# State's part of linear attention with 128 columns of weights on two row halves of the array

## The chip, the cores and the metric

The kernel runs on one core of one Trainium2 chip. The metric is the device time of one execution in microseconds (us), given as the median of several runs. One further execution was taken by the hardware profiler; the profile and the trace are of that one.

## The reference

Two stages follow each other. The first is causal linear attention with a decay for each head, over blocks of the sequence; the second mixes positions with a low-rank product and then runs a two-layer network on the channels.

```python
# q, k, v: (4, 8, 768, 64); lam: one decay for each of 8 heads
for b in range(nb):
    intra = einsum('bhic,bhjc->bhij', qb, kb) * Dmask
    intra = einsum('bhij,bhjd->bhid', intra, vb)
    inter = einsum('bhid,bhde->bhie', qb * lam_pow, kv_state)
    out[:, :, sl] = intra + inter
    kv_state = lam_block * kv_state + einsum('bhsd,bhse->bhde', kb * rev_pow, vb)
...
x = out.transpose(0, 2, 1, 3).reshape(B, S, H * D)      # (4, 768, 512)
xt = x.transpose(0, 2, 1)
u = x + (xt @ U @ V).transpose(0, 2, 1)                 # rank 32
return u + maximum(u @ w_ch1, 0) @ w_ch2                # 512 -> 2048 -> 512
```

All data are float32.

## The kernel before

The attention walks over 24 chunks of P = 128 positions (4 batches of NT = 6 chunks); `s` is the chunk, `c = s % NT` its place in the batch. All 8 heads of a chunk are worked on together, as HP = 4 pairs `a` of two heads `x`. In transposed tiles head `2a + x` of a pair lies on the partitions `half[x]`, that is 0 to 63 or 64 to 127. The kernel takes blocks of 128 positions where the reference takes 64, which gives the same sums.

For each chunk TensorE does this:

- `prep` (L358): transposes of q and k into `pqk`, copied by ScalarE (ACT) to `qt` and `kt` (L364).
- `scores` (L406): for each of 8 heads one product `kt` by `qt`, 64 rows of the array by 128 columns of weights, 128 moving columns, into the two PSUM banks of `pss`, bank `x` for the row half `x`. VectorE (DVE) multiplies by the mask (`masked`, L415) to `sm`.
- `intra` (L447): `sm` by `v` into `px`, with 64 columns of weights at a time (`t` is the half of the 128 positions).
- `state` (L425): `ks` by `v`, the sum for the next chunk, into `pkv`; DVE adds the faded old state and writes `kv` (L433).
- `inter` (L458): the part that comes from the state, `qs` (q times powers of the decay, made by GpSimd, L390) by `kv`, added into the same `px`. It is left out in the first chunk of a batch, where there is no state: 20 of the 24 chunks have it. Then ACT copies `px` to `x_nat` (L464).

`px` has two banks, one for each `x`; within a bank there are the 4 pairs by 64 output columns. `intra` starts the sums in a bank and `inter` adds to them.

Between these come the transposes and mixes of earlier chunks (L608, L559), and at the end of a batch the low-rank product (L474). The order is written by hand: `pieces` lists the functions chunk by chunk, and within one chunk TensorE runs, from the second batch on, `prep` of the next chunk, L608, L559, `intra`, `state`, `inter`, and `scores` of the next chunk. In the first batch `state` stands before `intra`. After the last chunk `inter` is followed by the first product of the network (L817) in place of scores. All loads and stores are issued by SyncE (SP): q, k and v from `load` (L279), where a new load waits until its buffer is free.

The attention fills the first 117 us. The rest of the time is the network: L817 and L827 for the first layer, L950, L952 and L954 for the second.

A float32 product is two instructions of TensorE and two weight loads, so the trace shows two records for each product of the attention. In the notation of the profile, "64*64" is rows by columns of the part of the array that a record uses, and PEld are the weight loads.

Of the kernel before, what the change touches and what calls it, by code (L numbers as in the profile page):

```python
# [18 lines left out]
def kernel(  # L19
# [28 lines left out]
    nc = tc.nc  # L48

    B, H, S, D = q.shape  # L50
    HP = H // 2
# [283 lines left out]
    st = {}  # L335
    kv = {}
    half = [slice(0, D), slice(D, P)]
# [114 lines left out]
    def inter(s):  # L452

        px = st[s]["px"][:, :, 0 : HP * D].rearrange("p x (a e) -> p x a e", a=HP)
        for a in range(HP if s % NT else 0):
            for x in range(2):
                for t in range(2):
                    nc.tensor.matmul(  # L458
                        out=px[half[t], x, a, :], lhsT=st[s]["qs"][half[x], a, half[t]],
                        rhs=kv[s][half[x], a, :], start=False, stop=(a == HP - 1),  # L460
                    )
        pool, tag = (att, "x10") if s % 10 == 5 else (x_pool, "x")
        xs[s] = pool.tile([P, C], FP32, tag=tag, name="x_nat")
        nc.scalar.copy(xs[s].rearrange("p (a x e) -> p x a e", a=HP, x=2), px)  # L464
        del st[s]
# [204 lines left out]
    def load_next(name, engine=nc.sync):  # L670
# [3 lines left out]

    run = {
        "prep": prep, "fade": fade, "scores": scores, "masked": masked, "inter": inter,
        "intra": intra, "state": state,
        "low": low, "low_rows": low_rows, "next_of_low": next_of_low, "mix": mix, "turn": turn,
# [375 lines left out]
```

## Time and profile before

| what | value |
|---|---|
| median of 3 runs | 667.36 us (666.33 to 668.0) |
| profiled execution, device time | 669.62 us |
| its span, first to last instruction | 667.8 us |
| granted TensorE clock | 1.00 |
| TensorE idle for "issue", 20 to 215 us | 4.0 us (1.6, 0.9, 0.8 and 0.7) |
| `inter` (L458), matmul records | 640, busy 14.7 us |
| `scores` (L406), matmul records | 384, busy 29.1 us |
| first product of the network (L817) starts | 117.36 us |

Busy time is the union of the records of a group; the ends of matmul records are modelled, so successive records overlap, and the time that a group costs is read from the start of its first record to the start of the next group's first. "Idle" is the time that the engine stood before a group, with what ended it; "issue" means that nothing in the profile explains it.

### The profile page before, as it was taken

How to read it: one execution, taken by the hardware profiler on the slowest of the kernel's cores; microseconds unless marked ns; L12 is line 12 of the kernel's file. 1: busy time of each engine (PE TensorE's matmuls, PEld its weight loads, DVE VectorE, ACT ScalarE, POOL GpSimd, SP SyncE). 2: the span in 40 equal slices, each digit the busy share in tenths (PEclk: the TensorE clock that was granted, in tenths of full speed). 3: DMA queues.
4: the chain of work that ended last, by engine and by line, in shares of the span. 5: the costliest groups of instructions: out<-in, count | busy, mean ns of one | idle time of the engine just before them, and what ended most of it. 6: DMA issues, size and time to landing. Idle time of an engine off the chain costs nothing.

```text
span 667.8 us, 13404 instructions
## 1 busy us (share of the span) xinstructions
PE 656.2 (98%) x5242; PEld 538.7 (81%) x5242; DVE 491.0 (74%) x862; ACT 280.4 (42%) x530; POOL 115.0 (17%) x98
## 2 busy tenths in 40 slices
PE   8899999999999999999999999999999999999997
PEld 7788988788888888888888887888888888888886
DVE  5578988878999777777797255786677776865864
ACT  4677885554555444444453121332322322322320
POOL 4465876330000000000000000030030300300300
PEclk9999999999999999999999999999999999999999
DMA  8999984355776655555578899764263453543531
GB/s 197 224 224 233 259 217 139 127 190 162 268 249 238 216 199 202 201 201 200 201 263 292 311 326 395 253 212 126 89 211 104 125 190 94 168 147 96 159 93 63
DMA packets 131776, 131.29 MB, mean 197 GB/s; under 512 B 81346, under 2 KB 89794, under 8 KB 131714
## 3 DMA queue, kind: packets, MB, share of 16 engines
q1 hardware_dynamic: 130512, 130.05, 62.2%
q8 instruction: 41, 0.67, 0.4%
q10 hardware_dynamic: 1202, 0.39, 0.2%
q14 instruction: 21, 0.17, 0.1%
HBM read 80.09 MB, written 50.33 MB: 195 GB/s over the span
## 4 chain that ended last, share of the span: by engine, by line
PE 95%; DMA 1%; DVE 1%; SPq 1%; issue 1%; ACT 0%; DVEq 0%; ACTq 0%
PE pz L817 27%; PE pz L950 13%; PE pz L952 13%; PE pd L827 13%; PE pd L954 13%; PE px L447 3%; PE pss L406 3%; PE px L458 2%; PE pqk L358 2%; DMA qraw<-in_q_dram 1%; PE pkv L425 1%; SPq L279 1%; PE pp L474 1%; PE pm L559 1%; PE put L590 1%
## 5 line engine op out<-in xcount | busy, mean ns | idle before, releaser
L817 PE MATMUL pz<-u_hl,w 128*128 128x512 f32 x768 | 190.0, 397 | 0.0
L817 PEld LDWEIGHTS pz<-u_hl,w 128*128 128x128 f32 x768 | 144.0, 188 | 35.2 <-ACT r L823 0.3
L952 PE MATMUL pz<-w_hl,m 128*128 128x512 f32 x384 | 151.1, 396 | 0.0
L950 PE MATMUL pz<-w_hl,m 128*128 128x512 f32 x384 | 150.9, 396 | 0.0
L954 PE MATMUL pd<-w_d,m 128*128 128x512 f32 x384 | 149.5, 396 | 0.0
L933 ACT ACTIVATE m<-mt 128x512 fp32r<-128x512 f32 x96 | 60.6, 632 | 196.6 <-PE pd L954 127.5
L979 POOL TENSOR_TENSOR o<-o,u 128x512 f32<-128x512 f32 x20 | 29.9, 1531 | 447.4 <-DMA rm<-r_d 291.4
L934 DVE SCALAR_TENSOR_TENSOR m<-rm,m 128x512 fp32r<-128x512 f32 x96 | 71.4, 745 | 47.3 <-ACT m L933 47.2
L832 DVE SCALAR_TENSOR_TENSOR r<-pd,r 128x512 f32<-128x512 f32 x96 | 61.8, 685 | 53.5 <-ACT r L823 43.5
L827 PE MATMUL pd<-u_d,w 128*128 128x512 f32 x384 | 98.6, 397 | 0.0
L823 ACT ACTIVATE r<-pz 128x512 f32<-128x512 f32 x96 | 52.1, 596 | 93.0 <-PE pz L817 92.3
L952 PEld LDWEIGHTS pz<-w_hl,m 128*128 128x128 f32 x384 | 72.3, 188 | 17.8 <-DVE m L934 0.2
L954 PEld LDWEIGHTS pd<-w_d,m 128*128 128x128 f32 x384 | 72.3, 188 | 17.7 <-DVE m L935 0.2
L950 PEld LDWEIGHTS pz<-w_hl,m 128*128 128x128 f32 x384 | 72.3, 188 | 17.6
L827 PEld LDWEIGHTS pd<-u_d,w 128*128 128x128 f32 x384 | 72.1, 188 | 17.3
L932 DVE TENSOR_SCALAR mt<-rm 128x512 uint32<-128x512 uint32 x96 | 46.1, 481 | 33.5 <-DMA rm<-r_d 33.2
L935 DVE SCALAR_TENSOR_TENSOR m<-m 128x512 fp32r<-128x512 f32 x96 | 69.1, 721 | 0.9
L415 DVE TENSOR_TENSOR sm<-pss,mask 128x512 f32<-128x512 f32 x48 | 30.9, 684 | 10.0 <-PE pss L406 9.7
L212 ACT CAST w<-wt 128x512 fp32r<-128x512 f32 x32 | 19.8, 620 | 30.6 <-DVE wt L209 23.4
L406 PE MATMUL pss<-qt,kt 64*128 64x128 f32 x384 | 29.1, 291 | 0.8 <-issue 0.7
L447 PE MATMUL px<-vraw,sm 128*64 128x64 f32 x768 | 27.8, 225 | 1.2 <-ACT x_nat L464 0.6
L447 PEld LDWEIGHTS px<-vraw,sm 128*64 128x64 f32 x768 | 24.9, 138 | 3.9 <-ACT x_nat L464 0.9
(96 smaller groups left out, 668.7 us busy)
## 6 DMA issues: line engine op xcount, KB each, us to landing
r_d<-r SPq DMA_DIRECT2D x96, 256.0 KB, 2.4
rm<-r_d SPq DMA_DIRECT2D x96, 256.0 KB, 2.7
words<-in_moe_w_ch_dram SPq DMA_DIRECT2D x30, 512.0 KB, 4.3
w_d<-w SPq DMA_DIRECT2D x16, 768.0 KB, 3.3
w_hl<-w_d SPq DMA_DIRECT2D x16, 512.0 KB, 6.4
vraw<-in_v_dram SPq DMA_DIRECT2D x24, 256.0 KB, 5.0
u_d<-x_nat SPq DMA_DIRECT2D x24, 256.0 KB, 4.1
u<-u_d SPq DMA_DIRECT2D x24, 256.0 KB, 4.1
```

Of the source, the lines that this page charges most:

```text
L406: nc.tensor.matmul(out=pss[:, x, a, :], lhsT=kt[half[x], a, :], rhs=qt[half[x], a, :], start=True, stop=True,)
L447: nc.tensor.matmul(out=px[half[t], x, a, :], lhsT=sm[:, x, a, half[t]], rhs=vr[:, 2 * a + x, :], start=(a == 0), stop=(alone and a == HP - 1),
L817: nc.tensor.matmul(out=acc[g][0], lhsT=w[:, n, ct, :], rhs=uhl[g][:, n, ct, :], start=(ct == 0 and n == 0), stop=(ct == CT - 1 and n == 1),)
L823: nc.scalar.mul(rs[g], acc[g][0], 4096.0 + 1.0)
L827: nc.tensor.matmul(out=acc[g][1], lhsT=w[:, 2, ct, :], rhs=ud[g][:, ct, :], start=(ct == 0), stop=(ct == CT - 1),)
L832: nc.vector.scalar_tensor_tensor(rs[g], acc[g][1], 4096.0, rs[g], ALU.mult, ALU.add)
L933: nc.scalar.activation(out=m[:, 0], in_=t, func=AF.Relu)
L934: nc.vector.scalar_tensor_tensor(m[:, 1], r, 0.0, hi, ALU.max, ALU.subtract)
L935: nc.vector.scalar_tensor_tensor(m[:, 2], hi, E, low, ALU.mult, ALU.subtract)
L950: nc.tensor.matmul(out=pz, lhsT=m[:, 0, cols], rhs=hl[:, 0], start=first, stop=False)
L952: nc.tensor.matmul(out=pz, lhsT=m[:, 1, cols], rhs=hl[:, 1], start=False, stop=end)
L954: nc.tensor.matmul(out=pd, lhsT=m[:, 2, cols], rhs=dd, start=first, stop=end)
```

## The change

In `inter`, the loop over `t`, the two halves of the 128 positions, goes away. One product now has the 128 positions of `qs` as its weights, on the 64 rows of half `x`, and writes all 128 partitions of bank `x`. Each product has the same 64 moving columns of `kv` as before. The number of products falls from 16 to 8 in each of 20 chunks. The part of the array that a product uses goes from 64 by 64 to 64 by 128, as it is in `scores`. What is computed is the same.

```diff
         for a in range(HP if s % NT else 0):
             for x in range(2):
-                for t in range(2):
-                    nc.tensor.matmul(
-                        out=px[half[t], x, a, :], lhsT=st[s]["qs"][half[x], a, half[t]],
-                        rhs=kv[s][half[x], a, :], start=False, stop=(a == HP - 1),
-                    )
+                nc.tensor.matmul(
+                    out=px[:, x, a, :], lhsT=st[s]["qs"][half[x], a, :],
+                    rhs=kv[s][half[x], a, :], start=False, stop=(a == HP - 1),
+                )
```

## The prediction

> **What bounds the kernel now.** I read four views, in this order: the page's busy rows, the groups by shape, the waits, and the order in time of one steady chunk of 128 positions. The page:
>
> ```profile
> span 667.8 us, 13404 instructions
> ...
> PE 656.2 (98%) x5242; PEld 538.7 (81%) x5242; DVE 491.0 (74%) x862; ACT 280.4 (42%) x530; POOL 115.0 (17%) x98
> ...
> PE 95%; DMA 1%; DVE 1%; SPq 1%; issue 1%; ACT 0%; DVEq 0%; ACTq 0%
> ```
>
> ```profile
> q8 instruction: 41, 0.67, 0.4%
> ```
>
> TensorE is the bound of the whole program, and 95% of the chain that ended last. All of the change lies in the attention, the first 117 us; from 117.36 on L817's products follow with no idle time, so what the attention loses or gains goes to the end unchanged. The q8 line matters later: 41 packets of 16,384 bytes. TensorE has 2 x 5242 records; at 64 bytes each that is 0.67 MB, so q8 is its instruction stream, in blocks of 256.
>
> The groups by shape (columns: busy us, mean ns | idle before). A float32 product has two records, so L458's x640 are 320 products.
>
> ```profile
> L406 PE MATMUL pss<-qt,kt 64*128 64x128 f32 x384 | 29.1, 291 | 0.8 <-issue 0.7
> ...
> L458 PE MATMUL px<-kv,qs 64*64 64x64 f32 x640 | 14.7, 225 | 1.0 <-issue 0.9
> ```
>
> ```profile
> L406 PEld LDWEIGHTS pss<-qt,kt 64*128 64x128 f32 x384 | 24.3, 193 | 2.6 <-issue 0.8 <-ACT kt L364 0.3
> L458 PEld LDWEIGHTS px<-kv,qs 64*64 64x64 f32 x640 | 11.6, 134 | 2.7 <-issue 1.2
> ...
> L358 PEld LDWEIGHTS pqk<-ident,qraw 64*128 64x128 f32 x192 | 9.6, 145 | 2.5 <-PE pss L406 1.1 <-issue 0.8 <-DVE kv L431 0.5
> ...
> L474 PEld LDWEIGHTS pp<-x_nat,u_w 128*32 128x32 f32 x192 | 5.0, 110 | 0.7 <-issue 0.4
> ```
>
> The reader is to see the load times: 110 ns for 32 columns of weights, 134 for 64, 193 for 128. The slope is (193 - 110)/96 = 0.86 ns a column (0.81 from the medians 188 and 110), so a load of 128 columns holds its part of the array about 107 ns, one of 64 about 54. L358 has 128 columns and only 145, but it is a transpose.
>
> One steady chunk on PE (start us, length us):
>
> ```profile
> 56.36 0.64 PE L425 MATMUL pkv<-vraw,ks 128*64 128x64 f32 x16
> 56.93 0.69 PE L458 MATMUL px<-kv,qs 64*64 64x64 f32 x32
> 57.55 1.16 PE L406 MATMUL pss<-qt,kt 64*128 64x128 f32 x16
> 58.55 0.41 PE L358 MATMUL pqk<-ident,qraw 64*128 64x64 f32 x8
> 58.79 0.42 PE L358 MATMUL pqk<-ident,kraw 64*128 64x64 f32 x8
> ```
>
> Ends are modelled, so I count from start to start: state's part (L458) takes 57.55 - 56.93 = 0.62 us, the scores 1.00. In single records L458 starts four together every 58 ns (88.148, 88.206, 88.265 us), 8 rounds, and then stands 147 ns between its last round (88.518) and the first of the scores (88.665): the switch of tiling. The scores start two together every 112 ns, with the first load, 107 ns, uncovered.
>
> The waits of the weight loads from 13 to 118 us:
>
> ```profile
> PEld pqk L358 <- issue: 2.4, 4, 1.8
> PEld px L458 <- issue: 1.2, 2, 1.1
> PEld pkv L425 <- issue: 1.0, 1, 1.0
> ...
> PEld px L447 <- ACT qt L364: 0.8, 2, 0.4
> PEld pss L406 <- issue: 0.8, 1, 0.8
> ```
>
> "Issue" is nothing that a semaphore explains. The large ones end at 21.04, 27.25, 52.12 and 108.88 us, each 2.2 to 2.5 us after a q8 packet began (18.78, 24.84, 49.64, 106.72), and the count of instructions executed at each is the same modulo 256. TensorE there ran out of instructions.
>
> **What the Trainium skill says.** "TensorE: Matmul & The Clock Gate", section "LDWEIGHTS (loading the stationary operand)": a load costs columns/1.2 ns, whatever the rows; that is 107 ns for 128 columns and 53 for 64, as the slope above has it. "TensorEngine Tiling (Array Packing)", section "Key Properties": changing the tiling mode drains the engine; here the 147 ns against a round of 58. "Runtime: NRT & Kernel Launch", section "Instruction fetch mechanics": instructions are refilled in blocks of 256 by the sequencer's own DMA queue, "mostly hidden"; the trace shows the blocks, and 4 us of PE idle where they weren't hidden.
>
> **The change part by part.** Per chunk, 16 products of 64x64 weights become 8 of 64x128; x still picks the row half and the PSUM bank, as in the scores. 320 products become 160, L458's records 640 become 320. No wait, tile or DMA moves: the qs and kv that it waits for are the same, and every other engine keeps its order.
>
> Removed: 8 rounds of 58 ns and the switch, 0.62 us. Added: 8 rounds in the scores' tiling. Two row halves start together, each with a load of 107 ns and 64 moving columns, which take 54 (the rounds of 58 stream the same 64). A product cannot start before its weights are in, and only one load ahead is seen in the trace, so the round is the load's: 107 to 112. I take the 112 of the scores, where load and stream are both 107. Together with the scores there are 16 rounds in one stream with one uncovered load: 16 x 0.112 + 0.10 = 1.89 us, against 0.62 + 1.00 = 1.62. So +0.27 us: half the products, each round twice as long, and the saved switch (about 0.09 + 0.10 with the uncovered load) gives back only a part. There are 20 such blocks (24 chunks less the first of each of 4 batches). 19 stand before scores: 19 x 0.27 = 5.1. The last stands before L817 (116.73 to 117.36, 0.63 us) and saves no switch: about 1.0, +0.4. Sum on PE: +5.5 us.
>
> Bounds of the round: below, 61 ns, that of L358's transposes, the only row with 128 columns of weights and 64 moving (8 records, 4 rounds, in 58.79 - 58.55 = 0.24 us); above, 116. At 61 a block would cost 1.89 - 8 x 0.051 = 1.48, -0.14 us, and the sum be about -2.5; at 116, +6.1. I take 112, since L358's loads are of another kind (145 ns at 128 columns).
>
> What hides part of it is idle time that PE already has:
> - Instruction supply. A steady chunk has 124 load-product pairs, 248 instructions, in 4.30 us (70.88 to 75.18), so a block of 256 lasts 4.4 us. After: 216 in 4.57, so a block lasts 5.4 us. The densest stretch, 64 instructions in 0.62 us, becomes 32 in 0.9. A fetch thus gets about 1 us more before TensorE runs dry. The late stalls are 0.83 (52), about 0.15 and 0.3 (98, 103) and 0.94 (108), all shorter than that or about it: I take 2.1 of 2.2 as gone.
> - The early stalls, 0.69 (21) and 1.64 (27). Were they gone, v would be late next: its tile for the chunk at 21.95 landed at 21.50, that for the chunk at 27.58 at 26.98. DMA is busy 0.9 to 1.0 there. I take 0.9 as recovered, and 0.2 of the wait for qraw at 16.59.
> - PE waits 0.27 us for the copy qt at 78.27, behind a DVE and ACT that are late; a PE that comes later waits less: 0.3.
>
> Sum: 5.5 - 2.1 - 1.1 - 0.3 = +2.0 us, or a little more where a fetch falls badly: +2.1. The profiled execution took 669.62 us (span 667.8, 1.8 around it); it becomes 671.7. That execution is 2.3 us over the median of 667.36 (its runs: 666.33 to 668.0); the same step on the median gives 669.5. Other engines get slack: the chunk grows from 4.30 to 4.57 us, and DVE, 94% busy from 70 to 90 us, falls below that. ACT's copy of px (L464) starts 0.27 us later in the chunk, still over a microsecond before intra of the next chunk needs px.
>
> **The rivals.**
> 1. Supply fully relieved: the early stalls go too, since the landings of v leave 0.5 to 1 us that I credited only in part, and slower loads shorten the DMA queue. 5.5 - 5.0 = about +0.5: 667.9. For it: the stalls add up to 4 us on PE and nearly 6 on its weight loads; against it: v.
> 2. Supply not relieved: the fetch begins 4 to 6 us after the block before it is entered in the early part, so it may be the DMA queue alone that sets it, and new blocks fall on new places. Then +4.3 to +5.5: 672.3.
> 3. The other side, faster: loads of 128 columns on two halves do not set the round, as for L358. One place, L458's round; price -0.14 us in each of 19 blocks, +0.0 in the last, -2.5 us with a supply that is relieved by 1 us: 663.9. The forecast of +2.0 is used up at a round of 112 - 2000/152 = 99 ns; below about 86 the kernel would be faster by what can be told. Against it: 188 ns loads of float32 and float32r in every row that is no transpose.
>
> **How the numbers follow.** A measurement tells a change from none at about 0.3%, 2.0 us. My case (+1.2 to +3.2, likeliest +2.1) has 0.45, split 0.27 slower and 0.18 within; rival 1 has 0.25, all within; rival 2 0.22, all slower; rival 3 0.08, faster. That makes slower 0.49, within 0.43, faster 0.08. The range 666.9 to 672.2 leaves out most of rival 3 and the worse half of rival 2.
>
> **What would show it.** Right: L458 x320 with loads near 188 ns and rounds of 107 to 112; L458 plus scores 1.85 to 1.92 us from start to start, with no gap above 112 ns between them; "issue" on PE from 13 to 118 us down from 4.0 to 1 to 2 us; the first L817 at about 119.4 instead of 117.36; nothing new after it. Wrong: rounds near 60 (rival 3); stalls as large as before (rival 2); or the first L817 before 118 (rival 1).

## The result, and the profile after

The changed kernel took 669.83 us (median of 5 runs, 668.61 to 670.67), the kernel before in the same comparison 666.99 us (5 runs, 666.33 to 668.0; the 667.36 us that the prediction starts from is the median of the first three of them). The ratio is 1.0040, with a 95% interval of 1.0023 to 1.0056: slower by 2.84 us. Two later comparisons with more runs of each gave 1.0005 (0.9990 to 1.0019) and 1.0024 (1.0011 to 1.0037). So the change costs between nothing and 0.4%, and which of these is measured goes with the kernel before, whose median was 666.99 us in the first comparison and 669.57 and 669.29 in the other two.

The page of the changed kernel, span, busy times and the queue of instructions:

```profile
span 668.0 us, 12764 instructions
...
PE 660.7 (99%) x4922; PEld 545.7 (82%) x4922; DVE 491.0 (74%) x862; ACT 280.6 (42%) x530; POOL 114.3 (17%) x98
...
q8 instruction: 39, 0.64, 0.4%
```

TensorE has 320 pairs fewer and is busy 4.5 us longer. q8 brings 39 blocks of instructions instead of 41. The groups by shape, first the products, then their loads (busy us, mean ns | idle before):

```profile
L406 PE MATMUL pss<-qt,kt 64*128 64x128 f32 x384 | 27.9, 286 | 0.1
L457 PE MATMUL px<-kv,qs 64*128 64x64 f32 x320 | 22.2, 278 | 0.0
```

```profile
L457 PEld LDWEIGHTS px<-kv,qs 64*128 64x128 f32 x320 | 19.4, 187 | 1.4
```

State's part (now L457) has half the records and is busy 22.2 us instead of 14.7. Its load went from 134 to 187 ns, the length of the scores' load. One steady chunk of the changed kernel in order of time (start us, length us):

```profile
55.98 1.11 PE L457 MATMUL px<-kv,qs 64*128 64x64 f32 x16
56.93 1.11 PE L406 MATMUL pss<-qt,kt 64*128 64x128 f32 x16
57.87 0.41 PE L358 MATMUL pqk<-ident,qraw 64*128 64x64 f32 x8
```

From start to start state's part takes 0.95 us (0.942 in the records) and the scores 0.94 (0.947), together 1.889 us where before took 1.62. In single records the products start two together every 112 ns, and the loads too; the first two records of the scores follow at the same pace, so the switch of tiling is gone. What is left beyond 16 rounds of 112 ns, 0.10 us, lies half before the second round of state's part (160 ns after the first) and half before the second of the scores (165 ns).

What TensorE waited for, 4 to 121 us, in the changed kernel (us in total, times, longest):

```profile
PE pkv L425 <- DVE sm L415: 0.9, 1, 0.9
PE px L447 <- issue: 0.3, 1, 0.3
PE px L447 <- DVE p_f L515: 0.3, 1, 0.3
...
```

The wait of 0.9 us is put down to DVE's `sm`, but `state` reads `ks` and v, and its v landed at 26.35 us, 0.14 before `state` started, the distance that waits named as waits for q or v have in other profiles (0.135 to 0.136): it is a wait for v. "Issue" was 4.0 us before and is 0.3 now. That the 4.0 us were instruction supply can be told from their place. Count all records of TensorE, of its loads and of the waits in its queue from the start of the program: the four stalls stand at places 193 and 194 of a block of 256, and so does a fifth one of 0.06 us, 4.2 us in all. This place is called the start of a block below. In the changed kernel no idle time stands there; its 0.3 us lies elsewhere in the count. The missing stalls pay back nearly the whole price in this pair of profiles: the first product of the network starts at 117.56 us instead of 117.36.

```profile
116.52 1.11 PE L457 MATMUL px<-kv,qs 64*128 64x64 f32 x16
117.56 1.67 PE L816 MATMUL pz<-u_hl,w 128*128 128x512 f32 x6
```

From there to the end it is 550.44 us in both (668.0 - 117.56 and 667.8 - 117.36), so nothing was gained or lost behind the attention. The two profiled executions thus differ by 0.2 us, the medians by 2.84. In this comparison the profiled execution of before, 669.62 us, is the odd one: it lies 1.6 us over the slowest of its five other runs. Beside the later experiments it is not: before's 102 runs there have a median of 669.4 us.

### The profile page after: what moved, and what is told of

Its sections match the earlier page's. It is cut to its first block, busy times and chain, and to the rows that moved or that the text cites. A ratio compares the mean times of both kernels' runs of the same rounds, so it can differ in the third digit from the quotient of the medians.

```text
span 668.0 us, 12764 instructions
## 1 busy us (share of the span) xinstructions
PE 660.7 (99%) x4922; PEld 545.7 (82%) x4922; DVE 491.0 (74%) x862; ACT 280.6 (42%) x530; POOL 114.3 (17%) x98
## 4 chain that ended last, share of the span: by engine, by line
PE 96%; DVE 1%; DMA 1%; ACT 1%; issue 0%; DVEq 0%
PE pz L816 27%; PE pz L951 13%; PE pd L826 13%; PE pz L949 13%; PE pd L953 13%; PE px L447 4%; PE pss L406 3%; PE px L457 3%; PE pqk L358 2%; PE pkv L425 1%; DMA vraw<-in_v_dram 1%; PE pm L558 1%; PE pp L473 1%; PE put L589 1%; PE pm L607 1%; PE idle L343 0%
```

## The experiments

Twelve further runs were made, three of the two kernels as they are and nine of edited ones. The theory: state's part is bound by the load of its weights, the price on TensorE is 5.5 us, and a part of it is paid back because the engine runs out of instructions less often. The main rivals: the round is set by something else than the load, or instruction supply has no part in it. A measure that leaves out the first loads of the program is used below: from the start of `state` in the second chunk (L425's second group) to the first product of the network, called the stretch.

**The kernel before, profiled again (no edit).**

> The kernel before, unchanged, profiled once more. Theory (the weight load sets the round of state's part, and a part of the loss is repaid by instruction supply): the first profile of before was a heavy one, 2.6 us above the median of its runs, and the excess is stalls of instruction supply. So this one has the network stage unchanged at 550.4 us from the first L817 to the end, and the first L817 at 114.5 to 116.5 instead of 117.36, with less than 4.0 us of issue on PE. Rival (the medians differ for a reason outside the attention): the first L817 at 117.4 again, issue 4.0, and the difference after it.

It took 666.89 us. The end of its attention and its waits from 13 to 118 us:

```profile
113.98 0.69 PE L458 MATMUL px<-kv,qs 64*64 64x64 f32 x32
114.60 1.67 PE L817 MATMUL pz<-u_hl,w 128*128 128x512 f32 x6
```

```profile
PE pqk L358 <- DMA qraw<-in_q_dram: 1.7, 2, 1.0
PE pkv L425 <- DMA vraw<-in_v_dram: 1.1, 2, 0.7
PE px L447 <- ACT qt L364: 0.4, 2, 0.3
PE px L447 <- issue: 0.3, 1, 0.3
...
```

The network starts at 114.60 us, 2.76 before that of the first profile, and takes 550.5 us to the end. The large stalls of supply are not there (0.2 us at the starts of blocks, instead of 4.2); the reader sees waits for loads of q and v in the early part instead. Against this execution the changed kernel's network starts 2.96 us later, close to the 2.84 us between the medians of the first comparison. The excess of the first profile fits stalls of supply, as the theory had it, and this says that they vary from one execution to the next. But this execution is among the shortest: 23 other runs of before, made with it, took 666.93 to 672.41 us, with a median of 669.26.

**Is the round the load's? Half the moving columns, and half the columns of weights.**

```diff
-                    out=px[:, x, a, :], lhsT=st[s]["qs"][half[x], a, :],
-                    rhs=kv[s][half[x], a, :], start=False, stop=(a == HP - 1),
+                    out=px[:, x, a, 0 : D // 2], lhsT=st[s]["qs"][half[x], a, :],
+                    rhs=kv[s][half[x], a, 0 : D // 2], start=False, stop=(a == HP - 1),
```

> The changed kernel with 32 of the 64 moving columns in each product of state's part: the contribution of the state to the other half of the output columns is left out. Theory (the load of 128 columns of weights sets the round): rounds stay at 112 ns, state's part at 0.94 us, the time within 1 us of the changed kernel. Rival (the round is the stream and its writes to PSUM): rounds of about 60 to 90 ns, state's part 0.5 to 0.75 us, the time 4 to 9 us less.

```diff
-                        rhs=vr[:, 2 * a + x, :], start=(a == 0), stop=(alone and a == HP - 1),
+                        rhs=vr[:, 2 * a + x, :], start=(a == 0),
+                        stop=((alone or t != x) and a == HP - 1),
...
-                    out=px[:, x, a, :], lhsT=st[s]["qs"][half[x], a, :],
+                    out=px[half[x], x, a, :], lhsT=st[s]["qs"][half[x], a, half[x]],
```

> The changed kernel with 64 instead of 128 columns of weights in each product of state's part, still 8 products on two row halves; the state's contribution to half of the positions is left out, and the switch of tiling before the scores is back. Theory (the round is the load, 0.83 ns a column): rounds of 58 ns, state's part 0.62 us up to the scores, scores 1.00, the first L816 at 111 to 113.5. Rival (the round belongs to two products at a time instead of four): rounds near 112, state's part near 0.95.

The first part of the second edit lets `intra` end the sums of the positions to which `inter` now adds nothing. A steady chunk with half the moving columns:

```profile
55.09 1.08 PE L457 MATMUL px<-kv,qs 64*128 64x32 f32 x16
56.01 1.14 PE L406 MATMUL pss<-qt,kt 64*128 64x128 f32 x16
56.98 0.41 PE L358 MATMUL pqk<-ident,qraw 64*128 64x64 f32 x8
```

and one with half the columns of weights:

```profile
52.59 0.68 PE L458 MATMUL px<-kv,qs 64*64 64x64 f32 x16
53.20 1.16 PE L406 MATMUL pss<-qt,kt 64*128 64x128 f32 x16
54.20 0.28 PE L358 MATMUL pqk<-ident,qraw 64*128 64x64 f32 x4
```

With half the stream, state's part plus scores takes 56.98 - 55.09 = 1.89 us, to the hundredth what the changed kernel takes; only the border between the two moves by 0.03 us, which would fit a last stream shorter by half. With half the columns and the same 16 records, state's part takes 0.61 us, about what four parts at a time took before (0.62). The round of state's part follows the columns of weights and not the stream, nor the number of products. The part of 64 by 128 as such doesn't set it either: the transposes (L358) use the same part, with 128 columns of weights and 64 moving, in rounds of 61 ns, and their loads are recorded with 145 ns instead of 187. Why those loads are shorter, no run here shows. As times these two runs are poor: 670.22 us for the first (expected within 1 us of the changed kernel, which it is), and 668.16 with the network at 115.34 us for the second, later than the expected 111 to 113.5. One wait of 2.8 us and one of 1.8 for a load of q are the reason, both seen once. The profile puts the first down to ACT, but the first half of DVE's `sm` ended at 50.85 us, just before `intra` started at 50.96; DVE had waited for a load of the network's weights until 47.83 and worked on them first.

**What does a switch of tiling cost? The state's sum put between.**

```diff
-        del st[s]
...
-        step += (both if s > NT else both[::-1]) + [("next_v", s), ("inter", s)]
+        if s > NT:
+            step += [("intra", s), ("inter", s), ("state", s), ("next_v", s)]
+        else:
+            step += both[::-1] + [("next_v", s), ("inter", s)]
```

> The changed kernel with the state's sum (L425) moved between state's part and the scores from the second batch on, so that the two no longer share a tiling in 12 chunks. Theory: each of these chunks pays two more switches, about 0.1 us each, and uncovered first loads of 54 and 107 ns: state's part 1.04 us up to its follower instead of 0.94, scores 1.00 instead of 0.95, the sum over TensorE 2 to 4 us more than the changed kernel, the first L817 at 119.5 to 122. Rival (a switch of tiling costs nothing of its own): less than 1 us more.

It took 675.76 us, one run, and the network starts at 123.49. A steady chunk:

```profile
57.40 1.11 PE L457 MATMUL px<-kv,qs 64*128 64x64 f32 x16
58.44 0.69 PE L425 MATMUL pkv<-vraw,ks 128*64 128x64 f32 x16
59.05 1.16 PE L406 MATMUL pss<-qt,kt 64*128 64x128 f32 x16
60.05 0.35 PE L358 MATMUL pqk<-ident,qraw 64*128 64x64 f32 x6
```

State's part is 1.04 us now, `state` 0.61 instead of 0.57, the scores 1.00 instead of 0.94 to 0.95. `intra`, which now has another tiling behind it, goes from 0.98 to 1.08. That is 0.1 for each of the two added switches where a stream must run out, and 0.05 for each first load of which less is covered. Over 12 chunks the records' differences (0.10 + 0.10 + 0.05 + 0.05) add up to 3.6 us. The whole was more than expected: the stretch is 111.07 us against 104.5 to 106.3 in three profiles of the changed kernel, with one further wait of 1.5 us that ends at 51.37; the rest of the excess is not explained. So one tiling is worth something; it is less than the longer load costs.

**Does the supply of instructions matter? Wide reads.** The kernel before and the changed one, each with:

```diff
-                in_=source[b, h : h + n, c * P : (c + 1) * P, :].rearrange("h p d -> p h d"),
+                in_=source.rearrange("b h s d -> (b h s) d")[s * P * H : (s + 1) * P * H].rearrange(
+                    "(p h) d -> p h d", h=H
+                )[:, h : h + n, :],
```

> The kernel before with q, k and v read in the same number of bytes but from consecutive addresses, packets of 2 KB instead of 256 bytes; the values reach other places of the tiles, so the computation is that of a permuted input. Theory: the DMA queues are short, blocks of instructions arrive in time, issue on PE after 13 us falls below 0.5 us, state's part plus scores stay at 1.62 us, the first L817 comes at 111.5 to 113.5, the time is 661.5 to 664.5. Rival (the stalls are not the DMA's doing): issue stays at 2 to 4 us and the time within 1 us of before, apart from the first loads.

> The changed kernel with the same wide reads, again a permuted input. Theory: with supply out of the way in both, the change costs its whole price on TensorE: 19 x 0.27 + 0.41 = 5.5 us over the run of before with wide reads (4.8 to 5.8). Rival (supply repays nothing, the price is smaller than counted): 2.8 us over it, as without wide reads.

Before took 665.29 us (664.19 to 666.39, 12 runs; 0.9945 of before, interval 0.9931 to 0.9959), the changed kernel 668.76 (667.59 to 669.32, 12 runs). Before's waits from 13 to 118 us:

```profile
PE pkv L427 <- issue: 0.7, 1, 0.7
PE px L449 <- issue: 0.7, 1, 0.7
PE px L449 <- ACT x_nat L466: 0.6, 2, 0.3
PE px L449 <- ACT qt L366: 0.4, 2, 0.3
PE pqk L360 <- issue: 0.2, 1, 0.2
PE px L460 <- issue: 0.2, 1, 0.2
```

The expectation failed in its size: 1.8 us of issue remain in before (1.7 at the starts of blocks), 0.3 in the changed kernel (none there), the time is over the 661.5 to 664.5 that were given, and the difference of the two is 3.47 us, not 5.5. Larger packets with the same bytes do not end the wait for instructions. Whether they shorten it is not shown, since before itself had 4.2 us in one profile and 0.2 in the other; what is shown is that before is 4 us faster with them than its median beside it (669.26), and spreads over 2.2 us instead of 5.5. The network of before starts at 113.31 us, within the 111.5 to 113.5 that were given; the stretch is 100.93 us in before and 103.35 in the changed kernel.

**Loads taken away.** Only the first three chunks load:

```diff
-    raw = {}
+    raw, kept = {}, {}
...
+        if s >= 3:
+            raw[s, name] = kept[s % 3, name]
+            return
-        t = raw_pool.tile(
+        t = kept[s, name] = raw_pool.tile(
```

> The kernel before in which only the first three chunks load q, k and v; the later chunks work on those data again, so 63 of 72 loads are left out and nearly no DMA stands beside the blocks of instructions. Theory: no stall of supply over 0.2 us after 20 us, state's part plus scores 1.62 us in every chunk, the first L817 at 109.5 to 112 us. Rival (a block of instructions takes its time whatever the DMA load): stalls of 0.5 us and more remain.

> The changed kernel with the same loads left out. Theory: the whole price of the change is seen, 5.0 to 5.7 us over the run of before without those loads, both in the time and in the first L816. Rival: 2 to 3.5 us, as with the loads.

> The kernel before without 63 of its 72 loads, a second time: in the pair without loads 1.0 us of the difference stood before state's part had run at all (chunk 1's pkv at 13.37 us in before, 12.39 in the changed kernel). Theory (the start is chance, and from chunk 1 on the change costs 4.4 us): the start falls elsewhere between 12.3 and 13.6, chunk 1's pkv to the first product of the network takes 98.9 us again (98.5 to 99.3), and the median time stays at 664 to 665. Rival (the changed kernel starts earlier of itself): the start at 13.3 to 13.5 again.

Before took 664.71 us (4 runs) and 664.83 (7 runs), the changed kernel 668.34 (20 runs, 668.0 to 669.69). From 20 to 118 us, first before, then the changed kernel:

```profile
PE px L450 <- DVE sm L418: 0.7, 2, 0.4
PE px L450 <- ACT qt L367: 0.7, 3, 0.3
PE px L450 <- ACT x_nat L467: 0.2, 1, 0.2
```

```profile
PE px L450 <- ACT qt L367: 0.4, 2, 0.2
PE px L450 <- DVE sm L418: 0.4, 1, 0.4
PE px L450 <- DVE p_f L518: 0.3, 1, 0.3
PE px L450 <- ACT x_nat L466: 0.2, 1, 0.2
```

There is no stall of supply on TensorE's products any more, in either: no idle time stands at the start of a block. With little DMA beside them (busy share 0.18 from 20 to 110 us, against 0.93), the blocks come in time. The network starts at 112.28 us in before, a little after the 109.5 to 112 that were given.

The difference of the times is 3.6 us and not the 5.0 to 5.7 that were expected. Two things make up the gap. Summed over the stretch, state's part takes 18.94 us instead of 12.50 and the scores 21.64 instead of 22.56: a price of 5.52 us, as counted. The stretch is 98.91 us in before, 98.92 in its second profile, and 103.33 in the changed kernel: 4.4 us more. So about 1.1 us of the price is hidden with nearly no DMA and no stall of supply in play, 1.0 of it in the time just before `intra`; what is seen to shrink is waits behind ACT and DVE (on the weight loads that for qt falls from 1.9 to 1.1 us, on the products those for qt and sm from 0.7 to 0.4 each). The rest, 1.0 us, stood before any state's part had run: `state` of the second chunk started at 13.37 us in before and at 12.39 in the changed kernel. The repeat was to tell whether that is chance. It started at 13.24, which settles neither side; in eleven other profiles of both kinds the start lies between 12.38 and 13.85 in no order. With wide reads it is the changed kernel that starts later (13.39 against 12.38), which speaks against the rival. What sets the start stays open.

The changed kernel's stretch without loads, 103.33 us, is the one with wide reads, 103.35, while before's 100.93 with wide reads lies 2.0 over its 98.91, nearly the 1.7 us of stalls at the starts of blocks there. So both pairs give 4.4 us as the price on TensorE once supply is out of the way.

**More instructions instead of fewer.** The other way to one tiling, from the kernel before:

```diff
-                nc.tensor.matmul(
-                    out=pss[:, x, a, :], lhsT=kt[half[x], a, :], rhs=qt[half[x], a, :],
-                    start=True, stop=True,
-                )
+                for t in range(2):
+                    nc.tensor.matmul(
+                        out=pss[half[t], x, a, :], lhsT=kt[half[x], a, half[t]],
+                        rhs=qt[half[x], a, :], start=True, stop=True,
+                    )
```

> The other way to have state's part and the scores in one tiling: before, with the scores' weights in two halves of 64 columns, so both use four parts of 64 by 64. Theory (the round is the longer of load and stream; a chunk has 280 instead of 248 instructions): state's part plus scores 0.05 + 8 x 0.058 + 8 x 0.112 = 1.41 us up to the last round and about 1.50 to the next transposes, which now pay a switch, against 1.62: 2 us less TensorE in all; but a block of 256 instructions lasts 3.9 us instead of 4.4, so stalls of supply grow by 1 to 5 us, and the kernel is within 0.3% of before or slower. Rival (supply is no limit): 2 us faster than before.

A steady chunk, and the waits from 13 to 118 us:

```profile
72.81 0.69 PE L459 MATMUL px<-kv,qs 64*64 64x64 f32 x32
73.33 1.06 PE L407 MATMUL pss<-qt,kt 64*64 64x128 f32 x32
74.31 0.40 PE L358 MATMUL pqk<-ident,qraw 64*128 64x64 f32 x6
```

```profile
PE pm L609 <- issue: 1.5, 1, 1.5
PE pqk L358 <- DMA kraw<-in_k_dram: 1.2, 1, 1.2
PE px L448 <- issue: 1.1, 3, 0.5
PE px L459 <- issue: 1.1, 2, 0.9
PE pqk L358 <- DMA qraw<-in_q_dram: 1.0, 2, 0.8
PE pqk L358 <- DVE sc L186: 0.9, 1, 0.9
PE pqk L358 <- issue: 0.8, 2, 0.5
...
```

State's part plus scores is 1.50 us, less than in both other kernels, as expected. And the kernel took 675.12 us, 1.0102 of before (1.0069 to 1.0135): issue is 4.5 us in these lines, and with two waits that stand at the starts of blocks too, though the profile puts them down to a load of k (1.2, but k landed only after TensorE had gone on) and to DVE (0.9), TensorE is idle for 6.9 us at 12 of 24 starts of blocks. The stretch is 107.54 us, 6.5 more than in before's second profile, where 0.2 us stood at the starts of blocks. It has 280 instructions in a chunk where before has 248 and the changed kernel 216. This is the plainest sign that instruction supply is a limit in the attention. It is also why it was no way to a faster kernel.

**The changed kernel again, in two further comparisons (no edit).**

> The changed kernel, unchanged, timed in the same job as the others, since the times of before spread from 666.9 to 672.4 us in the last job. Theory (the change costs a fixed 5.5 us of TensorE and takes away stalls that vary from execution to execution): the spread of the changed kernel is the smaller one, within 668 to 671 us, and its median lies 0.5 to 3 us over that of before. Rival (supply plays no part): both spread alike, and the difference is 5 us or more.

> The changed kernel once more, to set its spread beside before's in a further job. Theory: its median within 0.5 us of 670.0, before's between 667 and 669.7, whatever stalls before meets in this job; the ratio between 1.000 and 1.004. Rival (the first comparison was chance): ratio 1.000 or under, as in the last job.

| comparison | before: median, range, runs | changed: median, range, runs | ratio |
|---|---|---|---|
| first | 666.99, 666.33 to 668.0, 5 | 669.83, 668.61 to 670.67, 5 | 1.0040 (1.0023 to 1.0056) |
| second | 669.57, 667.37 to 675.12, 40 | 670.03, 668.8 to 675.69, 21 | 1.0005 (0.9990 to 1.0019) |
| third | 669.29, 666.24 to 672.27, 27 | 670.73, 669.1 to 672.94, 22 | 1.0024 (1.0011 to 1.0037) |

The changed kernel's median moves by 0.9 us over the three, before's by 2.6. In the second, 20 of 21 runs of the changed kernel lie within 668.8 and 671.4; before's reach from 667.4 to 675.1. The expectations for both runs held but for three margins: a difference of 0.46 where 0.5 to 3 was given, three runs over the 671 that was given as the end of the range (one at 675.69), and a median 0.73 from 670.0 where 0.5 was given. The last comparison alone speaks against the rival that the first difference was chance.

In the profiles of these two runs the stretch was 105.91 and 106.33 us, after 104.47 in the first; in before it was 104.29 and 101.08. The third's waits from 13 to 118 us:

```profile
PE pkv L425 <- POOL qs L390: 2.1, 1, 2.1
PE pkv L425 <- DMA vraw<-in_v_dram: 0.5, 1, 0.5
PE px L447 <- issue: 0.3, 1, 0.3
...
```

What is left is early waits for v. The one of 2.1 us, which the profile puts down to GpSimd's `qs`, is one too: `state` started at 28.13 us, and its v had landed at 27.99.

The time that TensorE stood idle at the starts of blocks, from 13 us to the network, in all profiles:

| instructions in a chunk | profiles | idle at the starts of blocks |
|---|---|---|
| 280 (scores in halves) | 1 | 6.9 us |
| 248 (before) | 2 | 4.2 and 0.2 us |
| 248, wide reads | 1 | 1.7 us |
| 248, loads left out | 2 | 0 |
| 216 (changed kernel, and its edits with all loads) | 7 | 0 in each |
| 216, loads left out | 1 | 0 |

Among the seven is the kernel with half the columns of weights, whose chunk is as quick as before's. In that profile it is the smaller number of instructions, and not a slower TensorE, that goes with blocks in time. What the table can't show is how much before was stalled in the second and third comparisons, since none of its executions there was profiled.

## Why the prediction was right, point by point

- *The round of state's part is the load's, 112 ns.* Right: 112 ns in the records, untouched by half the stream, and 58 with half the columns. The Trainium skill's price in "TensorE: Matmul & The Clock Gate", section "LDWEIGHTS (loading the stationary operand)", which gives an estimate of 107 ns for 128 columns, agrees: at the start of state's part the first two loads on one row half begin 108 ns apart (55.982 and 56.090 us). The transposes, with 128 columns in rounds of 61 ns, do not agree with it, and there the measurement decides.
- *State's part plus scores 1.89 us instead of 1.62, the last block +0.4, the sum +5.5.* Right: 1.889, +0.41 (1.038 instead of 0.625), and 5.52 us summed over the stretch of the pair without loads. The 0.10 us of uncovered load is there, but in two halves and not all at the start.
- *The late stalls, 2.1 us, go.* Right in the trace that it was read from, and more: issue on TensorE fell from 4.0 to 0.3 us, below the 1 to 2 that were given. But in the second profile of before they were nearly gone, and the five runs of the first comparison, 666.3 to 668.0 us, are as short as that one, so they probably had less to give back than the first profile. The step that was wrong is "the same step on the median gives 669.5": stalls that make one execution late by 2.3 us cannot be taken off the median too. In the later comparisons before's median is 669.3 to 669.6 us, as long as its first profile, and the change costs 0.46 and 1.44 us.
- *Of the early stalls 0.9 us, since v would be late next.* The mechanism is right: where the stalls are missing, TensorE waits for v and q (1.1 and 1.7 us in the second profile of before; 0.9, 2.4 and 2.6 for v in the three of the changed kernel). The size varies with the execution.
- *0.3 us less wait behind ACT and DVE.* Too small. With no loads and no stalls the difference is 4.4 us where the blocks cost 5.52, so about 1.1 is hidden, nearly all of it just before `intra`, where TensorE waits for DVE's `sm` and ACT's `qt`. That DVE was busy for 94% of the time from 70 to 90 us could have been a hint. That the waits behind it shrink because it is nearly a second bound is argued, and no run here varied its load.
- *The total.* 669.83 us measured, 669.5 predicted. That it is so close is in part luck. For the profiled execution itself the prediction was 671.7 us, +2.1, and it became 669.83, +0.2; for the median the same +2.1 stands against 2.84, 0.46 and 1.44 us in the three comparisons. For the median of the first, two errors of size went opposite ways: too much taken off for stalls, too little for ACT and DVE. Rival 1, where supply pays back all, is what the first pair of profiles looks like, and its own sign is there (the network before 118 us: 117.56), and the second comparison; rival 2, where it pays back nothing, was seen nowhere (the changed kernel's network started at 118.81 and 119.22 us in its other two profiles). Rival 3, rounds near 60 ns, is excluded.

## What to carry to other kernels

Halving the number of products saves nothing where each keeps its weights' columns busy twice as long: compare columns of weights per part of the array and columns streamed, and take the longer. Here that is 112 ns for 128 columns of weights and 64 or 32 moving, 58 for 64 and 64, and 110 for the halved scores with 64 and 128; the transposes, 61 ns with 128 and 64, do not follow it. A stall that the profile calls "issue" and that ends 2.2 to 2.5 us after a packet of instructions began varied here from 4.2 to 0.2 us between two executions of one kernel; look at a second profile before you take it off a median. Where instruction supply is tight, count the instructions of a change beside its engine time.

## What was not expected of the hardware

Thirty-two more instructions in each chunk (280 for 248), with 0.12 us less work on TensorE in state's part plus scores, made the kernel 1% slower. With 216 instructions in a chunk none of eight profiles has a stall at the start of a block. The same kernel before, unchanged, spread over 7.8 us (667.37 to 675.12) in one comparison. Reading the same bytes in packets of 2 KB instead of 256 bytes gave only 0.55%, and did not end the stalls (1.7 us in its one profile); leaving the loads out did.
